# Fp32 opening matmuls, fewer filler matmuls, another order of ko and fo, and shifted batch 1 steps in an attention-and-MoE kernel

## The chip, the cores and the metric

The kernel runs on one core of one Trainium2 chip. The metric is device time in microseconds (us) of that core. Comparisons are of the time of one kernel to that of the kernel before on the same chip in the same rounds. The profiled span (first to last instruction) is some 1.8 us shorter than the device time of the same execution.

## The reference

```python
kv  = einsum('bhsd,bhse->bhde', k, v)          # b 8, h 8, s 576, d 64
out = einsum('bhsd,bhde->bhse', q, kv)
rms = sqrt(mean(out*out, axis=-1, keepdims=True) + 1e-6)
x   = (out / rms * g_norm) -> [4608, 512]
h   = x @ w_in                                 # [512, 2048]
y   = (h * sigmoid(1.702 h)) @ w_out           # [2048, 512]
```

## The kernel before

Tokens go through in nine blocks of 512. Block 0 needs the attention of batch 0 first, and while it runs all weights are still on their way from HBM. The attention of batch b + 1 is spread, as "steps", over the matmuls of block b. GpSimd issues the loads that cast fp32 to fp16, in this order: q, k, v of batch 0 for head pairs 1 to 3 (pair 0 comes through SyncE), `w_in` in five pieces, `w_out` and batch 1's q, k, v interleaved.

Names used below: a pair is two of the eight heads. ko is one of the four blocks of 128 rows of `w_in`, one for each pair; fo is one of the 16 blocks of 128 columns of h. The group is fo 0 to 5 of block 0: 24 matmuls, whose order is part of the change. "The last product" is the scaled attention output of pair 3, which the ko 3 matmuls read. A kv step of batch 1 is k^T v of one pair, for which VectorE first packs k. A gate is the activation on ScalarE. TensorE "stands" by the time that a matmul starts later than 0.216 us after the 512-column matmul before it, which is the spacing in these traces when nothing is waited for (stands at kv steps are counted the same way).

```python
load_w_in(0, 4, 0, 2)      # fo 0-3, ko 0-1
load_w_in(0, 4, 2, KO)     # fo 0-3, ko 2-3   <- "the second w_in half" below
load_w_in(4, GROUP)        # fo 4-5
load_w_in(GROUP, 10)
load_w_in(10, FO)
# ... (cut)
def busy(n):               # filler: zero matmuls into a PSUM tile nobody reads
    for _ in range(n):
        nc.tensor.matmul(idle_ps, kvb[1][:, 0, :],
                         kvb[1].rearrange("p c r -> p (c r)"), start=True, stop=True)

busy(12)                   # the opening
a0.q(0); busy(2); a0.kv(0) # transposes of q, then k^T v, of head pair 0
# ... g_col (cut)
busy(2)
a0.out(0); a0.q(1); a0.kv(1); a0.sums(0)
a0.out(1); a0.q(2); a0.rs(0)
busy(1)
a0.kv(2); a0.sums(1); a0.apply(0)
busy(1)
a0.out(2); a0.rs(1); a0.q(3); a0.kv(3); a0.sums(2); a0.apply(1)
a0.out(3); a0.rs(2); a0.apply(2)
busy(3)
d0 = Hidden(0)             # h = x @ w_in; xT[ko] is what apply(ko) writes
for fo in range(4):        # ko 0; after fo 2: a0.ss(3), a0.apply(3) -> "the last product"
    d0.mm(0, fo, ...)
for ko in (1, 2):
    for fo in range(4): d0.mm(ko, fo)
for ko in range(KO - 1): d0.mm(ko, 4, ps_o, "o")
for fo in range(GROUP - 1): d0.mm(KO - 1, fo)
for ko in range(KO): d0.mm(ko, GROUP - 1, ps_o, "o")
# ... (cut) in block 0's output matmuls, after matmul number n, counted from 0:
at2((25, 27, 42, 43)[c], of(1, "kv", c))
o = (31, 34, 50, 53)[c]
at2(o, of(1, "out", c))
```

## Time and profile before

| | before |
|---|---|
| time, 6 runs beside the changed kernel | 287.00 us median (286.87 to 287.51) |
| profiled span | 284.9 us |
| TensorE busy | 279.1 us |
| v of pair 3, landing | 12.77 us |
| second w_in half, landing | 16.47 us |
| first output matmul of block 0 | 28.73 us |
| first hidden matmul of block 1 | 46.77 us |

From 46.77 us on TensorE waits for no load (one stand of 0.13 us at 47.3). The prediction shows and reads the lines of this profile.

### The profile page before, as it was taken

Reading aid. Unit: us, or ns where it says so; the run is one execution under the profiler, and the core shown is the slowest. Engines: PE = TensorE matmul, PEld = TensorE weight load, DVE = VectorE, ACT = ScalarE, POOL = GpSimd, SP = SyncE. Lnnn points to the kernel's source line nnn. Section 1 sums busy time; section 2 is a strip of 40 time slices with the busy share of each in tenths; the row PEclk is TensorE's granted clock in tenths of the full one; section 3 lists DMA queues with packets and bytes.
Section 4 is the critical chain, followed back from the end, with each engine's and each line's share of the span. In section 5 each row is a group of like instructions: output and inputs, shape, how many; then the busy total and the mean of one; then the engine's idle time right before and its main releaser. Section 6 shows DMA issues by size and latency. Waiting matters only on the chain.

```text
span 284.9 us, 4354 instructions
## 1 busy us (share of the span) xinstructions
PE 279.1 (98%) x1717; PEld 135.1 (47%) x1717; DVE 118.9 (42%) x230; ACT 156.1 (55%) x273; POOL 57.1 (20%) x82
## 2 busy tenths in 40 slices
PE   8899999999999999999999999999999999999995
PEld 2444544455445544554455445544454444444443
DVE  2550666527661657157713852286327400110001
ACT  2697439766575646574458536763666365016400
POOL 8931461111211121112011401130002100000000
PEclk9999999999999999999999999999999999999999
DMA  8999999995589358953797279925401410012022
GB/s 176 200 207 204 205 249 239 242 268 105 122 165 254 60 147 161 242 90 69 224 208 138 38 216 200 184 39 184 83 2 37 120 66 0 0 69 81 0 74 74
DMA packets 54070, 38.76 MB, mean 136 GB/s; under 512 B 31219, under 2 KB 50931, under 8 KB 53923
## 3 DMA queue, kind: packets, MB, share of 16 engines
q0 software_dynamic: 14960, 15.58, 33.5%
q1 hardware_dynamic: 38688, 22.39, 30.2%
q10 hardware_dynamic: 402, 0.52, 0.5%
q8 instruction: 13, 0.21, 0.3%
q14 instruction: 7, 0.05, 0.1%
HBM read 36.73 MB, written 9.44 MB: 162 GB/s over the span
## 4 chain that ended last, share of the span: by engine, by line
PE 93%; POOL 2%; DMA 2%; DVE 1%; issue 0%
PE hT L434 44%; PE o L471 42%; PE kvp L223 3%; DMA vbuf<-in_v_dram 2%; PE outR L287 2%; PE oh L503 1%; POOL kraw L91 1%; PE ss L335 1%; POOL qraw L91 1%; DVE kpad L214 1%; PE outT L255 0%; POOL vbuf L91 0%; PE q L412 0%; PE outT L266 0%; PE idle L558 0%
## 5 line engine op out<-in xcount | busy, mean ns | idle before, releaser
L471 PE MATMUL o<-w_out_sb,gT 128*128 128x512 f16 x560 | 130.7, 379 | 0.0
L443 ACT ACTIVATE gT<-hT 128x512 f16<-128x512 f32 x144 | 84.5, 599 | 76.5 <-PE hT L434 76.4
L434 PE MATMUL hT<-xT,w_in_sb 128*128 128x512 f16 x512 | 116.2, 379 | 0.0
L434 PEld LDWEIGHTS <-w_in_sb 128*128 128x128 f16 x576 | 54.6, 98 | 62.3 <-DMA w_in_sb<-in_moe_w_in_dram 0.5
L471 PEld LDWEIGHTS <-gT 128*128 128x128 f16 x560 | 52.9, 98 | 56.2 <-issue 0.2
L481 DVE COPY osb<-o 128x512 f32<-128x512 f32 x20 | 13.8, 690 | 62.4 <-PE o L471 62.4
L319 POOL TENSOR_TENSOR x<-xr,g_all 128x512 f16<-128x512 f32 x12 | 15.2, 1270 | 71.2 <-DVE xr L312 47.2
L214 DVE COPY kpad<-kraw 64x576 f16<-64x576 f16 x56 | 25.0, 446 | 2.0 <-DMA kraw<-in_k_dram 0.7
L298 DVE TENSOR_REDUCE sum<-sq 128x8 f32<-128x512 f16 x24 | 15.8, 679 | 19.9 <-ACT sq L295 19.9
L236 DVE CAST kvb<-kvp 64x128 f16<-64x128 f32 x28 | 8.1, 288 | 36.5 <-PE kvp L223 36.4
L312 DVE TENSOR_TENSOR xr<-outR,sum 128x512 f32<-128x512 f32 x24 | 15.5, 686 | 11.1 <-ACT sum L309 11.1
L112 POOL DMA_DIRECT2D kraw<-in_k_dram x16 | 9.9, 624 | 48.8 <-DVE kpad L214 42.8
L112 POOL DMA_DIRECT2D vbuf<-in_v_dram x16 | 9.7, 608 | 33.9 <-PE kvp L223 29.3
L319 DVE TENSOR_TENSOR x<-xr,g_all 128x512 f16<-128x512 f32 x12 | 15.2, 1267 | 0.7
L295 ACT ACTIVATE sq<-outR 128x512 f16<-128x512 f32 x24 | 13.6, 591 | 2.0 <-PE outR L287 1.6
L223 PEld LDWEIGHTS <-kpad 128*128 128x128 f16 x252 | 11.0, 98 | 7.0 <-DVE kpad L214 0.9
L434 PE MATMUL hT<-x_rem,w_in_sb 128*128 128x512 f16 x64 | 14.0, 379 | 0.0
L275 ACT ACTIVATE sq<-outT 128x512 f16<-128x512 f32 (+1 forms) x16 | 7.7, 481 | 10.4 <-PE outT L255 9.0
L481 ACT COPY osb<-o 128x512 f32<-128x512 f32 x15 | 8.7, 581 | 6.3 <-DMA out_dram<-osb 6.3
L223 PE MATMUL kvp<-vbuf,kpad 128*128 128x64 f16 x252 | 11.9, 193 | 0.1
L308 ACT ACTIVATE sum<-sum,eps_t 128x16 f32<-128x16 f32 x12 | 3.7, 308 | 15.0 <-DVE sum L298 14.9
L337 ACT ACTIVATE ln<-ss,eps_t 128x512 f32<-128x512 f32 (+1 forms) x16 | 9.4, 586 | 4.3 <-PE ss L335 4.1
(62 smaller groups left out, 141.5 us busy)
## 6 DMA issues: line engine op xcount, KB each, us to landing
qf<-in_q_dram SPq DMA_DIRECT2D x5, 1024.0 KB, 9.0
out_dram<-osb SPq DMA_DIRECT2D x10, 512.0 KB, 2.9
kraw<-in_k_dram POOLq DMA_DIRECT2D x12, 288.0 KB, 6.9
vbuf<-in_v_dram POOLq DMA_DIRECT2D x12, 288.0 KB, 5.5
w_out_sb<-in_moe_w_out_dram POOLq DMA_DIRECT2D x3, 512.0 KB, 14.4
out_dram<-osb SPq DMA_DIRECT2D x6, 192.0 KB, 5.5
qf<-in_q_dram POOLq DMA_DIRECT2D x1, 1024.0 KB, 11.1
out_dram<-osb SPq DMA_DIRECT2D x1, 1024.0 KB, 3.8
```

Source lines behind the costliest of these rows:

```text
L112: nc.gpsimd.dma_start(out=raw[n][l * PH : (l + 1) * PH, c0:c1, 0 : NH * D], in_=srcs[n][b].rearrange("(c l) (p j) d -> l p c (j d)", l=2, ...
L214: nc.vector.tensor_copy(out=kpad[r, c, :, l * D : (l + 1) * D], in_=kraw[r, c, 0 : NH * D].rearrange("p (j d) -> p j d", j=NH),)
L223: nc.tensor.matmul(self.kvp[:, c, :], kpad[:, c, j, :], vbuf[:, c, j * D : (j + 1) * D], start=(j == 0), stop=(j == NH - 1),)
L295: nc.scalar.activation(sq, t, AFT.Square)
L298: nc.vector.tensor_reduce(out=self.sum2[:, j % 2, :], in_=sq.rearrange("p (h d) -> p h d", h=H), op=ALU.add, axis=mybir.AxisListType.X,)
L312: nc.vector.tensor_mul(xr[:, i], self.o[j + i].rearrange("p (h d) -> p h d", h=H), s2[:, i, :].unsqueeze(2).to_broadcast([P, H, D]),)
L319: (nc.vector if i else nc.gpsimd).tensor_mul(self.x16[:, j + i, :].rearrange("p (h d) -> p h d", h=H), xr[:, i], g_all.unsqueeze(1).to_bro ...
L337: nc.scalar.activation(ln[:, 0:n], t[:, 0:n], AFT.Ln, bias=eps_t, scale=1.0 / D)
L434: nc.tensor.matmul(self.h[fo], w_in_sb[:, ko, fo * P : (fo + 1) * P], self.x[:, ko], start=(ko == 0), stop=(ko == KO - 1),)
L443: nc.scalar.activation(self.gT[:, fo, :], self.h[fo], AFT.Gelu_apprx_sigmoid)
L471: nc.tensor.matmul(os[mo], gT[:, fo, mo * P : (mo + 1) * P], w_out_sb[:, fo, :], start=(fo == 0), stop=(fo == FO - 1),)
L481: copy(osb[:, mo, :], os[mo])
```

## The change

Its intent, as far as the code tells: to release TensorE's clock with fewer instructions, to take out filler, to run each fo of the first group in a simpler order, and to give batch 1's kv matmuls more time to be fed.

```diff
+    zeros = const.tile([P, SM], F32)
+    nc.vector.memset(zeros, 0.0)
...
-    busy(12)
+    for _ in range(3):
+        nc.tensor.matmul(idle_ps, zeros[:, 0:P], zeros, start=True, stop=True)
...
     a0.rs(0)
-    busy(1)
     a0.kv(2)
     a0.sums(1)
     a0.apply(0)
-    busy(1)
     a0.out(2)
...
-    busy(3)
+    busy(1)
...
-    for ko in (1, 2):
+    for ko in range(1, KO):
         for fo in range(4):
             d0.mm(ko, fo)
-    for ko in range(KO - 1):
-        d0.mm(ko, 4, ps_o, "o")
-    for fo in range(GROUP - 1):
-        d0.mm(KO - 1, fo)
-    for ko in range(KO):
-        d0.mm(ko, GROUP - 1, ps_o, "o")
+    for fo in range(4, GROUP):
+        for ko in range(KO):
+            d0.mm(ko, fo, ps_o, "o")
...
-                at2((25, 27, 42, 43)[c], of(1, "kv", c))
-                o = (31, 34, 50, 53)[c]
+                at2((27, 28, 42, 43)[c], of(1, "kv", c))
+                o = (32, 35, 50, 53)[c]
```

## The prediction

> **What bounds the kernel now.** I read the page first (busy shares, clock, chain), then the chain in order of time, then the waits, and last the timeline of the first 48 us, where the change lies.
>
> ```profile
> span 284.9 us, 4354 instructions
> PE 279.1 (98%) x1717; PEld 135.1 (47%) x1717; DVE 118.9 (42%) x230; ACT 156.1 (55%) x273; POOL 57.1 (20%) x82
> ...
> PE 93%; POOL 2%; DMA 2%; DVE 1%; issue 0%
> ```
>
> TensorE is busy 98% of the span and is 93% of the chain that ended last. Of the 576 hidden and 560 output matmuls nothing changes, so the change can only win or lose idle or filler time of TensorE, and only where that time is on the chain. The chain in order of time says where that is not so:
>
> ```profile
> 7.23 5.54 DMA vbuf<-in_v_dram
> 12.90 0.40 PE kv L372 x12
> 13.68 0.39 PE outT L255
> 14.07 0.65 PE idle L558 x3
> 14.71 0.65 PE hT L434 x3
> ```
>
> Up to 12.9 us the chain is not TensorE but GpSimd issuing loads and the landing of the last v block of batch 0 (issued 7.23, landed 12.77). The twelve opening zero matmuls are not in it. After 12.9 us the three zero matmuls are in it, but see what follows them:
>
> ```profile
> 1.27 4.92 PE L558 MATMUL idle<-kvb 128*128 128x512 f16 x12 [1.27 <-DVE one_t L185]
> 6.16 0.31 PEld L389 LDWEIGHTS <-qraw 96*64 96x64 f16 x12 [0.49 <-ACT qraw L549]
> 12.90 0.38 PE L372 MATMUL kv<-vbuf,kraw 96*64 96x64 f16 x12 [0.70 <-DMA vbuf<-in_v_dram]
> 16.51 0.76 PEld L434 LDWEIGHTS <-w_in_sb 128*128 128x128 f16 x5 [0.35 <-DMA w_in_sb<-in_moe_w_in_dram]
> 17.00 0.75 DVE L349 SCALAR_TENSOR_TENSOR xT<-outT,g_col,rs 128x512 f16<-128x512 f32 x1 [0.88 <-ACT rs L343]
> 35.52 0.32 PEld L223 LDWEIGHTS <-kpad 128*128 128x128 f16 x9 [0.36 <-DVE kpad L214]
> 36.47 0.32 PEld L223 LDWEIGHTS <-kpad 128*128 128x128 f16 x9 [0.58 <-DVE kpad L214]
> ```
>
> At 6.16 the first transposes wait for ScalarE's cast of q; at 12.90 TensorE has stood 0.70 us for a load; at 16.51 a weight load waits for the second half (ko 2 and 3) of the first w_in load. The trace has that load landing at 16.469, issued at 8.615 from GpSimd, with nothing before it that waits on TensorE. At 36.47 the second kv step of batch 1 waits for VectorE's packing of k. No later stretch shows TensorE waiting, so a shift there reaches the end one for one.
>
> **What the Trainium skill says.** (1) TensorE: Matmul & The Clock Gate, Part 1, "What's actually happening": the array runs at 1.2 GHz after idleness and 2.4 GHz after about one busy window of 3.4 us. This case agrees: the opening matmuls start 0.426 us apart up to 5.09, the one at 5.514 takes 0.300, and later 512-column matmuls start 0.216 apart. (2) FP8 and Floating Point Precision, "TensorE Precision Notes": true fp32 takes four passes. The trace of before has fp32 matmuls only for g_ps: two instructions recorded as four load and four matmul records, one column wide, so it shows the split into two records but not the time. (3) VectorE: DVE Perf Modes, "Zero memsets can be issued as uint32 (trn2)": one cycle per element. Here 256 words took 0.27 us and 1152 words 1.02, so about 0.84 ns a word more: it agrees. (4) DMA: Bandwidth & Descriptors, "Queues, rings and completion order": descriptors are consumed in ring order. The landings of GpSimd's loads do come in order of issue here (14.07, 16.47, 17.11, 19.64, 23.37 for the five w_in loads), so moving TensorE's work should not move them.
>
> **Part 1, the opening.** Twelve fp16 matmuls of 512 columns go; three fp32 ones of four passes come: 12 x 512 column steps either way, so the same array time. The new memset of 512 words (estimate from the two measured ones: 0.27 + 256 x 0.84 ns = 0.48 us) stands where the 0.27 us memset stood, so TensorE starts near 1.50 instead of 1.27. If the clock still doubles near 5.69 (0.173 us into the matmul at 5.514, from its 0.300), 4.19 us cold cover 5028 of 6144 steps and the other 1116 take 0.47 us warm: end 6.16, just where the q transposes start today on ScalarE's cast. Cost on the chain: nothing, and even 0.5 us late would fit in the 0.70 us stand at 12.90 plus the fillers taken out below.
>
> **Part 2, single fillers before kv 2 and out 2.** 0.43 us of TensorE goes, ahead of the 12.77 landing: nothing on the chain.
>
> **Part 3, three fillers to one after out 3.** out 3 starts at 13.68 as before (DMA-led). The hidden matmuls start at 14.12 instead of 14.55, just after the landing at 14.07. Three of them end at 14.77; the sum matmul for pair 3 then waits for ScalarE's square (14.23 + 0.60 = 14.83, about 0.05 to start) and goes at 14.88, not 15.20: 0.32 us earlier. Log, exp and the last product follow: log 15.62 to 15.30, exp 16.34 to 16.02, product 17.00 to 16.68, ending near 17.43. TensorE does fo 3 and ko 1 (five matmuls) from 15.10 to 16.17 and then stands until the landing: ko 2 starts at 16.515 **as before**. The 0.43 us taken out turns into a wait for w_in.
>
> **Part 4, the order of ko and fo.** From 16.515 on both orders have 16 matmuls of the group left. Before, ko 3 came after seven of them, at 18.04, and the last product, done at 17.75, was hidden. Now ko 3 comes after four, which would be at 17.39; the last product is there at 17.43 + 0.05 = 17.48. So a stand of 0.09 us: the group ends 0.09 us later (its last matmul at 19.86 instead of 19.76). fo 4 needs the load of 17.11, in time. The gates start earlier (about 17.95 instead of 18.45, behind the 1.28 us table load) but ScalarE is not what ends last here. The later loads for fo 6 and 10 (19.64, 23.37) are in before 20.07 and 23.64. Sum of the front: **+0.09 us**.
>
> **Part 5, batch 1 steps.** Before: the kv step of pair 0 after step 25 loses 35.521 - 35.486 = 0.035 us; pair 1 after step 27 could go at 36.226 and goes at 36.478 when its packing is done: 0.252 us lost. Now two more output matmuls (2 x 0.216) come ahead of pair 0, which then starts at 35.92 without a wait; after one more, pair 1 could go at 36.39 and still waits to 36.478, 0.084 us. Everything from there has one more output matmul behind it at the same moment. The out step moves from 31 to 32, so four matmuls still cover the two copies of kv (36.95 to 37.54), and it still goes at 37.615. kv of pairs 2 and 3 would go near 40.42 with their v landed at 40.09 and their packing done at 40.09: still fed. Gain: **-0.216 us**.
>
> **Sum.** +0.09 - 0.216 = -0.13 us of 287.01: **286.9 us**.
>
> **Rivals.** (a) The fp32 opening is slower than four passes, or doesn't release the clock: the start would slip. For: no duration of an fp32 512-column matmul is in this trace. Against: the replacement of 12 by 3 is just the skill's factor of four. Absorbed up to about 0.7 us; if each took twice as long, some 4 us would go, of which over 3 us reach the end: 290. (b) The taken-out 0.86 us of fillers (four at 0.216) come back in full, with part 5: 287.01 - 0.86 - 0.22 = 285.9. For: three of the five fillers concerned are in the chain at 14.07. Against: the wait at 16.51 for a load that TensorE doesn't lead. (c) ko 3 waits longer, because the sum of pair 3 isn't earlier than today (15.20): the product would end at 17.75, ko 3 at 17.80, 0.41 us lost in the front and 287.2 in all. (d) The later kv steps meet another wait (v for pairs 2 and 3 lands 0.3 us ahead of need): the gain of part 5 goes, 287.1.
>
> **Range and chances.** All but (a) lie between 285.9 and 287.2, with the three timed runs of before 0.25 us apart. I weigh (b) little. Range 286.4 to 287.4. Two per cent is 5.7 us: only a gross form of (a) reaches it. Faster by over 2%: 0.003; within 2%: 0.987; slower by over 2%: 0.01.
>
> **What would show it.** In the changed trace: six fp32 matmul records in the opening, each near 0.85 us apart while cold, ending about 6.2; the kv matmuls of pair 3 still at 12.90 behind v; a weight load at 16.5 behind w_in with a longer idle than 0.35; the last product near 16.7; a short gap of TensorE before ko 3; then the kv step of pair 1 with under 0.1 us of stand. Wrong if the opening ends after 7 us, if ko 2 starts well before 16.5, or if the first output matmul comes earlier than in before (28.73).

## The result, and the profile after

The changed kernel took 286.89 us (median of 6, 286.75 to 287.15), the one before 287.00 us in the same rounds. The ratio is 0.9994, 95% interval 0.9981 to 1.0007: the same. (A ratio is the mean time of one kernel's fast runs over that of the other's of the same rounds, so not quite the ratio of the medians quoted.) A difference of 0.11 us lies far inside that interval, so the sum can't be checked by time; its terms can be checked in the traces, where each is a shift between two events of one execution.

The page of the changed kernel, span, TensorE row and chain by engine:

```profile
span 285.0 us, 4335 instructions
PE 278.8 (98%) x1707; PEld 134.9 (47%) x1707; DVE 119.2 (42%) x231; ACT 156.2 (55%) x273; POOL 57.2 (20%) x82
...
PE 93%; DMA 3%; POOL 3%; issue 0%; DVE 0%
```

TensorE has 0.3 us less to do, and the span is no shorter. The chain that ended last, in order of time, says why (changed kernel; start, duration, what):

```profile
8.01 0.72 POOL w_in_sb L168
8.73 7.80 DMA w_in_sb<-in_moe_w_in_dram
16.53 0.05 issue
16.58 5.48 PE hT L436 x24
```

Before, the chain ran through the landing of v at 12.77 and then through TensorE. Now the landing of the second w_in half at 16.53 is in it, and all TensorE work before 16.58 has dropped out of the chain. Of the 0.43 us of fillers taken out after out 3, 0.09 became a stand at the sum of pair 3 and 0.28 a longer stand ahead of ko 2 (0.304 us, before 0.020).

The lines of the timeline that answer to those shown of before (start, duration, engine, line, operation; in brackets the engine's idle time before it and what ended it):

```profile
1.54 5.06 PE L570 MATMUL idle<-zeros 128*128 128x512 f32 x6 [1.54 <-DVE zeros L152]
6.54 0.45 PE L391 MATMUL q<-ident,qraw 96*64 96x96 f16 x12
13.02 0.38 PE L374 MATMUL kv<-vbuf,kraw 96*64 96x64 f16 x12 [0.62 <-DMA vbuf<-in_v_dram]
16.57 0.76 PEld L436 LDWEIGHTS <-w_in_sb 128*128 128x128 f16 x5 [0.63 <-DMA w_in_sb<-in_moe_w_in_dram]
16.78 0.75 DVE L351 SCALAR_TENSOR_TENSOR xT<-outT,g_col,rs 128x512 f16<-128x512 f32 x1 [0.54 <-ACT rs L345]
23.80 0.33 PEld L436 LDWEIGHTS <-w_in_sb 128*128 128x128 f16 x3 [0.40 <-DMA w_in_sb<-in_moe_w_in_dram]
36.74 0.32 PEld L225 LDWEIGHTS <-kpad 128*128 128x128 f16 x9 [0.23 <-DVE kpad L216]
```

The weight load at 16.57 waits 0.63 us where it waited 0.35. The last product starts at 16.78 instead of 17.00. At 23.80 a matmul now stands for its load: the last w_in load (fo 10 to 15) landed at 23.76, not at 23.37, when only the weight load had waited (0.20 us at 23.41). Only one kv wait is left, at 36.74, of 0.23 us for the weight loads, where there were two of 0.36 and 0.58.

TensorE's shift at the first hidden matmul of block 1, in parts, each from starts of single instructions:

| part | before | after | difference |
|---|---|---|---|
| second w_in half lands | 16.469 | 16.532 | +0.063 |
| from there to the group's last matmul | 3.294 | 3.420 | +0.126 (stand at ko 3 of 0.129) |
| from there to the first output matmul | 8.966 | 9.044 | +0.078 (stand at fo 10 of 0.068) |
| from there to block 1 | 18.044 | 17.830 | -0.214 |
| first hidden matmul of block 1 | 46.773 | 46.826 | +0.053 |

Rest of the kernel: 234.496 us before to the last matmul's start, 234.498 after. So this execution lost 0.053 us; of that, 0.063 and most of 0.078 are landings that fell later in it.

### The profile page after: what moved, and what is told of

The parts are those of the page before. It is cut to its first block, busy times and chain, and to the rows that moved or that the text cites. A ratio compares the mean times of both kernels' runs of the same rounds, so it can differ in the third digit from the quotient of the medians.

```text
span 285.0 us, 4335 instructions
## 1 busy us (share of the span) xinstructions
PE 278.8 (98%) x1707; PEld 134.9 (47%) x1707; DVE 119.2 (42%) x231; ACT 156.2 (55%) x273; POOL 57.2 (20%) x82
## 4 chain that ended last, share of the span: by engine, by line
PE 93%; DMA 3%; POOL 3%; issue 0%; DVE 0%
PE hT L436 43%; PE o L473 42%; DMA w_in_sb<-in_moe_w_in_dram 3%; PE kvp L225 3%; PE outR L289 2%; PE oh L505 1%; POOL qraw L91 1%; POOL kraw L91 1%; POOL vbuf L91 1%; PE ss L337 1%; PE q L414 0%; PE outT L268 0%; PE outT L257 0%; POOL w_in_sb L168 0%; POOL ident L154 0%
```

## The experiments

Each kernel was built and timed beside the kernel before in five rounds; all gave correct results. "Low clock" counts the executions whose mean granted TensorE clock was 0.996 or less.

| run | median us (range) | before, same rounds | ratio, 95% interval | low clock |
|---|---|---|---|---|
| changed, first rounds | 286.89 (286.75 to 287.15) | 287.00 | 0.9994, 0.9981 to 1.0007 | 0 of 6 |
| e1_opening | 287.21 (286.68 to 289.87) | 287.38 | 1.0009, 0.9978 to 1.0039 | 0 of 6 |
| e2_front | 287.33 (287.06 to 288.84) | 287.38 | 1.0010, 0.9988 to 1.0032 | 2 of 6 |
| e3_steps | 286.84 (286.54 to 287.07) | 287.38 | 0.9985, 0.9970 to 1.0000 | 0 of 5 |
| e4_old_order | 286.87 (286.54 to 288.49) | 287.38 | 0.9995, 0.9974 to 1.0016 | 1 of 6 |
| e5_changed_again | 286.84 (286.61 to 288.69) | 287.03 | 1.0004, 0.9984 to 1.0024 | 1 of 6 |
| e6_singles_back | 286.91 (286.54 to 287.27) | 287.03 | 0.9996, 0.9983 to 1.0009 | 0 of 5 |
| e7_no_fillers | 286.99 (286.37 to 287.53) | 287.03 | 0.9998, 0.9986 to 1.0010 | 1 of 6 |
| e8_combined | 287.10 (286.80 to 287.54) | 287.03 | 1.0005, 0.9993 to 1.0017 | 0 of 5 |
| e9_cut_loads | 286.65 (286.47 to 287.32) | 286.93 | 0.9991, 0.9979 to 1.0004 | 0 of 5 |
| e10_no_opening | 288.40 (287.32 to 289.36) | 286.93 | 1.0042, 1.0021 to 1.0063 | 0 of 6 |
| e11_six | 288.76 (288.09 to 289.21) | 286.93 | 1.0056, 1.0042 to 1.0070 | 0 of 5 |
| e12_fillers_only | 286.88 (286.80 to 288.16) | 286.93 | 1.0002, 0.9987 to 1.0017 | 1 of 6 |

Only e10 and e11 differ from before beyond their interval. The rest is read from traces. What makes single traces hard to compare is the landings: the gap between the landings of the first and second w_in half was 2.2 to 2.8 us in five traces (before, changed, e5, e6, e12) and 1.2 to 1.3 us in the other seven in which that load was whole (e1 to e4, e7, e10, e11), with no pattern by kernel that I could find: the changed kernel had the late landing both times. So I measure stands and stretches inside one trace.

### e1: the opening alone

```diff
-    busy(12)
+    for _ in range(3):
+        nc.tensor.matmul(idle_ps, zeros[:, 0:P], zeros, start=True, stop=True)
     # and the memset of zeros
```

> The kernel before with the fp32 opening alone. Theory (the opening lies in the slack before the landing of v): six records about 0.85 us apart, the first q transposes 0.0 to 0.5 us later than the 6.16 us of before, but the kv matmuls of pair 3 still within 0.1 us of the landing of their v, and from there nothing moved other than by landings; time ratio to before 1.000 within 0.001. Rival (the start is on the path): the shift of the transposes is still there at the kv matmuls of pair 3, after their v has landed, and the time goes up by the same 0.3 to 0.5 us.

Six records, the cold ones 0.853 us apart. q started at 5.92, earlier than before and not later as expected, because this time the clock was released at 4.81 us and not at 6.05 as in the changed kernel. kv of pair 3 started 0.136 us after its v landed, over the 0.1 expected, but as before (0.135). The form of the opening doesn't reach the end: theory held in what matters. One execution of 289.87 us with its clock at 0.999 has no explanation here; its trace was not taken.

### e2: fillers and order alone

```diff
-    busy(1)        # ahead of kv 2
-    busy(1)        # ahead of out 2
-    busy(3)
+    busy(1)
     # and the new order of ko and fo
```

> The kernel before with the five fillers cut to one and the new order of ko and fo alone; the opening and the batch 1 steps are those of before. Theory (the landing of the second w_in half leads ko 2): the filler time turns into a stand of TensorE in front of ko 2, the first ko 2 weights load within 0.06 us of that landing, ko 3 stands 0.08 to 0.15 us for the last product; from landing to the end of the group 3.55 to 3.65 us against 3.51 in before; time 0.0 to 0.2 us above before. Rival (fillers come back): ko 2 starts 0.3 us or more before 16.5 and the time falls by 0.4 us or more.

Neither theory nor rival described this trace. Stretches of it: length, TensorE busy (instructions), granted clock, DMA share, GB/s.

```profile
10.00:12.00 2.00, 1.49 (x27) 1.00 1.31 199
12.00:13.60 1.60, 0.90 (x14) 0.99 1.21 185
13.60:17.00 3.40, 3.33 (x19) 0.50 1.32 202
17.00:19.00 2.00, 2.00 (x10) 1.00 1.24 208
```

From 13.58 to 16.99 us the clock stood at half. The kernel before has 2.00 us busy in the stretch from 10 to 12 and a clock of 1.00 in all of these. So the fillers may have a use that I had not seen: in this execution the clock fell just after the stretch in which they were gone, and the span was 287.0 us. That they would have kept the clock, this trace alone doesn't show. The second w_in half landed early here (16.09), and TensorE didn't wait for it; ko 3 stood 0.446 us for the last product.

### e3: the batch 1 steps alone

```diff
-    at2((25, 27, 42, 43)[c], of(1, "kv", c));  o = (31, 34, 50, 53)[c]
+    at2((27, 28, 42, 43)[c], of(1, "kv", c));  o = (32, 35, 50, 53)[c]
```

> The kernel before with the two kv and two out steps of batch 1 shifted, nothing else. Theory: the stand ahead of the kv matmuls of pair 1 falls from 0.25 to about 0.08 us and that of pair 0 from 0.035 to 0, so the stretch from the first output matmul to the first hidden matmul of token block 1 is 0.216 us shorter than the 18.04 us of before; time 0.1 to 0.3 us less. Rival (the gain is lost at a later step, such as kv of pair 2 waiting for its v): that stretch stays at 18.04 us within 0.05.

The waits of the weight loads for VectorE's packing (total us, times, longest), in the kernel before:

```profile
PEld L223 <- DVE kpad L214: 0.9, 2, 0.6
```

and in e3:

```profile
PEld L223 <- DVE kpad L214: 0.2, 1, 0.2
```

Stands of the matmuls: 0.083 us at pair 1 and none at pair 0. The stretch from first output matmul to block 1 was 17.828 us: 0.216 us less than 18.044, as computed. The theory held to the hundredth of a microsecond in the trace. The medians differ by 0.54 us, more than the steps can give; that is within the noise of these rounds.

### e4: the changed kernel with the old order

```diff
-    for ko in range(1, KO):                      # all of fo 0-3, then fo 4 and 5
+    for ko in (1, 2): ...                        # ko 3 of fo 0-3 after ko 0-2 of fo 4
```

> The changed kernel with the old order of ko and fo put back: everything else as changed. Theory (the new order exposes the last product): the stand ahead of ko 3 of 0.13 us in the changed kernel goes to 0, the group ends 3.5 us after the landing of the second w_in half instead of 3.6, unless the load for fo 4 lands too late for its new place 4 matmuls after ko 2 starts (it landed 0.64 us after the ko 2 load in before and 0.96 in the changed kernel; fo 4 comes 0.87 us after ko 2 starts). Time 0.0 to 0.2 us less than the changed kernel. Rival: the order was changed because the fo 4 load is late: then TensorE stands there instead and nothing is won, or up to 0.1 us lost.

ko 3 no longer stood. But fo 4 stood 0.068 us for its load (landed 17.15), fo 10 stood 0.075 us for its load (23.39), and an output matmul stood 0.123 us at 37.42 for the piece of w_out with fo 8 to 11 (37.38). The group ended 6.72 us after the landing of v (before 6.99, changed 7.07), yet the stretch from output matmul to block 1 grew to 17.951. Part of the gain was given back at the next landing. e3 is the closer comparison: it has the same order and the same steps, all five fillers, and an early second half too. From the landing of v to the group's end e4 is 0.25 us shorter (6.718 against 6.964), and to the first hidden matmul of block 1 only 0.04 (33.720 against 33.758). So with an early half, 0.25 of the 0.43 us of fillers after out 3 did come back, and was then lost at the next landings. Theory held on ko 3, and the rival's wait came too, smaller.

### e5: the changed kernel again

> The changed kernel once more, untouched, to have it beside the others on one chip. In the front-only run the clock fell to half for one 3.4 us window near 13 to 17 us in the profiled execution (mean clock 0.993), and 1 of 6 runs of the old-order one had 0.994. Theory (the removed fillers also kept the array busy enough): the changed kernel shows it too, 0 to 3 of 6 runs at a mean clock of 0.996 or less and 1 to 2 us longer, the rest at 286.7 to 287.2. Where the second w_in half lands early (1.3 us after the first, as in the last four runs), theory for the front: ko 3 still starts 0.05 us after the last product, so the group ends 7.0 to 7.1 us after the landing of v for pair 3, as in before (6.99). Rival (only the landing held it): the group ends 6.75 us or less after it.

One of six executions had a clock of 0.994 and took 288.69 us; the other five lay at 286.61 to 287.08. So the changed kernel has the loss of clock too. In the profiled execution the second w_in half landed late, at 16.63, 4.06 us after v, and TensorE stood 0.717 us for it:

```profile
16.68 1.69 PE L436 MATMUL hT<-xT,w_in_sb 128*128 128x512 f16 x7 [0.55 <-DMA w_in_sb<-in_moe_w_in_dram]
```

(The bracket counts from the modelled end of the matmul before.) ko 3 did not stand at all, since the last product was done before ko 2 was through. The early-landing case that the expectation speaks of didn't come up here. It came in e7.

### e6: the two single fillers put back

```diff
     a0.rs(0)
+    busy(1)
     a0.kv(2)
     ...
+    busy(1)
     a0.out(2)
```

> The changed kernel with the two single fillers ahead of kv 2 and out 2 put back. Theory (those two hold the clock through the stretch of 10 to 13 us): no run at a mean clock of 0.996 or less, and in the trace nothing from the landing of v for pair 3 on moved by more than 0.05 us against the changed kernel. Rival (the loss of clock comes from the two fillers taken out after out 3, or from chance): the low-clock runs are as frequent as in the changed kernel.

No low clock in five. From the landing of v to the end of the last product 4.646 us, in the changed kernel 4.646: the two fillers cost nothing, as the landing of v comes after them. Later landings did move things by more than the 0.05 us expected: an output matmul stood 0.146 us at 37.59 for w_out, and the stretch to block 1 was 17.973 us (17.830). Five executions don't prove that the clock is safe: at one in six, none of five would come up by chance two times in five.

### e7: no filler after the opening

```diff
     a0.q(0)
-    busy(2)
     a0.kv(0)
     ...
-    busy(2)
     a0.out(0)
     ...
-    busy(1)
     d0 = Hidden(0)
```

> The changed kernel with every filler after the opening taken out (two pairs and the last one), so that the suspected loss of clock is exaggerated; the opening of three fp32 stays. Theory: at least 2 of 6 runs at a mean clock of 0.996 or less and 1 us or more longer than the others; median 287 to 289. Rival (fillers don't matter for the clock once it is released): no such run, and the time within 0.2 us of the changed kernel.

One low clock of six, not two or more, and that execution took 287.53 us, not 1 us more: my expectation missed. More filler taken out didn't make the loss more frequent. The trace showed the front with an early second w_in half (15.68), in a line of the timeline:

```profile
17.84 1.46 PE L436 MATMUL hT<-xT,w_in_sb 128*128 128x512 f16 x6 [0.27 <-DVE xT L351]
```

ko 3 waits for the last product, 0.434 us by matmul starts, and the group ends 7.075 us after v landed. So with the new order the front has two ceilings: the landing, and, when that is early, the last product. The freed time is gone either way.

### e8: a version from the findings so far

```diff
     # changed kernel, single fillers back, old order of ko and fo, and
-    load_w_in(0, 4, 2, KO)
+    load_w_in(0, 4, 2, 3)
+    load_w_in(0, 4, 3, KO)
-    load_w_in(10, FO)
+    load_w_in(10, 12)
+    load_w_in(12, FO)
-    at2((27, 28, 42, 43)[c], of(1, "kv", c));  o = (32, 35, 50, 53)[c]
+    at2((27, 29, 42, 43)[c], of(1, "kv", c));  o = (33, 36, 50, 53)[c]
```

> A version made from the findings: the changed kernel with the single fillers back, the old order of ko and fo, the second w_in half cut in two loads and the last w_in load cut in two (fo 10-11, fo 12-15), and kv of pair 1 one step later (outs too). Theory: the stand ahead of the kv matmuls of pair 1 is under 0.02 us (0.085 in the changed kernel), no stand at fo 10, the group ends 0.2 to 0.3 us sooner after v of pair 3 landed than in before (6.99), so 0.4 to 0.6 us under before in all and no run at a low clock: 286.3 to 286.7. Rival: the load for fo 4 (17.1 to 17.5) takes the place of ko 3 as the stand and the front gains 0.1 or less.

The kv stand of pair 1 went to 0.000 and fo 10 didn't wait. But fo 4 stood 0.292 us for its load, and this line came up:

```profile
37.73 0.59 PE L475 MATMUL o<-w_out_sb,gT 128*128 128x512 f16 x2 [0.31 <-DMA w_out_sb<-in_moe_w_out_dram]
```

An output matmul stands 0.469 us by matmul starts for fo 8 of w_out, landed at 37.69. The group ended 6.945 us after v: the rival was right, and 0.3 us of gain in the steps ran into the next load. No faster than before.

### e9: two more loads cut

```diff
-    load_w_in(4, GROUP)
+    load_w_in(4, 5)
+    load_w_in(5, GROUP)
-            load_w_out(8, 12)
+            load_w_out(8, 10)
+            load_w_out(10, 12)
```

> The combined version with two more loads cut in two: w_in for fo 4-5 and w_out for fo 8-11. In the combined run the TensorE gains ran into the landing of w_out fo 8-11 (stand of 0.469 us at 37.73) and of w_in fo 4-5 (0.292 at 17.33). Theory (one landing after another paces the first 48 us, and the first half of a cut load lands earlier by about half of the time that load takes): both stands fall below 0.1 us, the group ends 0.2 us or more sooner after v of pair 3 than the 6.99 us of before, and the stretch from first output matmul to token block 1 is 17.72 to 17.80 us (17.83 in the changed kernel): 286.3 to 286.7, 0.3 to 0.6 us under before. Rival (cutting only moves the wait to the next landing, or costs on the queue): one of the stands is still 0.2 us or more, or another of that size appears, and the time stays within 0.2 us of before.

The trace is that of the slowest of the five executions (287.32 us). The two stands fell to under 0.02 us (fo 4) and 0.129 us (at 38.34, for the second half of the cut w_out load). The group ended 6.64 us after v. But the kv matmuls of pair 2 now stood 0.214 us, and the waits of TensorE name it:

```profile
PE kvp L228 <- DMA vbuf<-in_v_dram: 0.2, 1, 0.2
```

v of batch 1's second half landed at 40.79, 0.13 us before that step; later, in block 1, another kv step stood 0.318 us at 57.0. The median, 286.65, is the lowest and 0.28 us under before; its interval includes 1. The stretch to block 1 was 18.073 us, not 17.72 to 17.80. So the rival was right about the wait that moves on, and the theory about the group's end and, nearly, the two stands (0.129 is over its 0.1).

### e10: no opening at all

```diff
-    for _ in range(3):
-        nc.tensor.matmul(idle_ps, zeros[:, 0:P], zeros, start=True, stop=True)
```

> The changed kernel without its three opening matmuls. Theory (the opening only releases the clock, its form doesn't matter): the matmuls of batch 0's attention run at half clock (two zero matmuls 0.427 us apart), the clock is released late, between 9 and 18 us, kv of pair 3 starts 0.2 us or more after its v landed, and the time is 1 to 3 us above the changed kernel. Rival (the opening isn't needed): kv of pair 3 starts within 0.15 us of the landing and the time is within 0.3 us of the changed kernel.

The timeline of TensorE:

```profile
7.07 1.03 PE L560 MATMUL idle<-kvb 128*128 128x512 f16 x2
14.65 0.52 PE L374 MATMUL kv<-vbuf,kraw 96*64 96x64 f16 x12
16.44 1.26 PE L436 MATMUL hT<-xT,w_in_sb 128*128 128x512 f16 x3
```

The trace is of a slow execution of the six (289.22 us). Zero matmuls are 0.40 to 0.43 us apart, kv of pair 3 starts 1.83 us after its v (landed 12.82), and the clock is released at 17.34. Time 288.40, ratio 1.0042: the opening is worth 1.5 us. With e1, which changed the form alone, it is the release, and not the form, that counts.

### e11: six fp32 matmuls

```diff
-    for _ in range(3):
+    for _ in range(6):
```

> The changed kernel with six opening fp32 matmuls in place of three, to find the slack of the opening. Theory (array time of four passes at the released clock, 0.43 us a record, and a slack of about 0.7 us before v of pair 3): the twelve records end near 8.8 us, the q transposes start 2.2 to 2.6 us later than the 6.2 to 6.6 of the changed kernel, kv of pair 3 starts 1.2 to 2.0 us after the landing of its v instead of 0.13, and 0.9 to 1.8 us of that reach the end. Rival (the front has far more slack): less than 0.4 us reaches the end.

```profile
1.54 7.82 PE L570 MATMUL idle<-zeros 128*128 128x512 f32 x12 [1.54 <-DVE zeros L152]
9.29 0.45 PE L391 MATMUL q<-ident,qraw 96*64 96x96 f16 x12
14.79 0.35 PE L374 MATMUL kv<-vbuf,kraw 96*64 96x64 f16 x12
```

Records are 0.853 us apart cold and 0.430 after the release at 6.41. q starts 2.75 us later than in the changed kernel, a little more than expected because the release came later than assumed. kv of pair 3 starts 2.03 us after its v instead of 0.135. On the clock of the trace it starts at 14.793 instead of 13.018, 1.775 us later (its v landed 0.12 us sooner): the slack of the opening is 2.753 - 1.775 = 0.98 us. The time grew by 1.83 us over before (medians), a hair over the upper end expected. What goes beyond the slack reaches the end.

### e12: the fillers alone

```diff
-    busy(1)        # ahead of kv 2
-    busy(1)        # ahead of out 2
-    busy(3)
+    busy(1)
```

> The kernel before with the five fillers cut to one, its order, opening and steps kept: the fillers by themselves. So far a mean clock of 0.994 or less came in 5 of 30 executions of kernels without the two single fillers and in none of 43 with them whose clock is on record. Theory (those fillers guard the clock, and the freed time is taken by landings): 0 to 3 of 6 runs at 0.996 or less, 1 to 2 us longer; the others within 0.3 us of before; in the trace the kv and fo 4 or fo 10 stands show where the freed 0.43 us went. Rival (the freed time is kept): the runs at full clock 0.3 us or more under before.

Here the second w_in half landed late, at 16.68. Weight loads:

```profile
16.72 0.78 PEld L434 LDWEIGHTS <-w_in_sb 128*128 128x128 f16 x5 [0.86 <-DMA w_in_sb<-in_moe_w_in_dram]
```

TensorE stood 0.527 us at ko 2 (before 0.020), and that is where the freed time went, not to the later stands that I expected. The group ended 3.295 us after the landing, before 3.294. That isolates Part 3 of the prediction for a late second half: fillers taken out with nothing else change nothing from the landing on. One of six executions had a clock of 0.994 and 288.16 us; the other five took 286.80 to 286.92.

### What the clock counts say

The kernels that lack the two single fillers and keep an opening of ordinary length (changed twice, e2, e4, e7, e12) had 6 low-clock executions of 36. Those that have them (before, e1, e3, e6, e8, e9) had none of 59. I formed the idea on e2 and e4, so the fair count starts after them: 3 of 18 (e5, e7, e12) against 0 of 37 (before in two calls, e6, e8, e9). If both kinds were alike, all three would fall in the first kind with a chance of (18 x 17 x 16) / (55 x 54 x 53) = 3%. That fillers guard the clock is therefore likely and not proved. It is at odds that e7 had no more of it than e5, and that e10 and e11, which also lack the singles, had none of 11; I left them out for their opening, and with them the 3% becomes 8%. Nor do the counts separate the two singles from the two fillers taken out after out 3: the kernels with the singles and without those two (e6, e8, e9) have only 15 executions.

The half-clock window was seen in one trace only, and this trace holds a hint. In e2's clock records the first stretch at full clock lasts 6.827 us and the one at half clock 3.413, half of it. Cut every trace from its release on in steps of that length, up to 24 us: the step just ahead of the fall is the emptiest of all, with 2.23 us of TensorE busy; the next emptiest is in e3, which kept its clock (2.36). In e2 and then e3:

```profile
10.17:13.58 3.41, 2.23 (x39) 1.00 1.26 192
4.86:8.27 3.41, 2.36 (x35) 1.00 1.24 186
```

The two singles would have added some 0.43 us to e2's step (an estimate, two at 0.216). Where a step falls depends on when the clock was released, so this would fit a loss in some executions only; with one fall traced it is not shown.

## Why the prediction was right

- **Part 1, the opening.** Right in effect. The memset took 0.485 us (0.48 worked out; 64, 256, 512 and 1152 words took 0.112, 0.272, 0.485 and 1.018, so 0.83 ns a word, and whether that is one cycle, as the page that the prediction cites has it, no run here shows) and TensorE started at 1.54 (1.50). Records came 0.853 us apart. The end near 6.16 didn't come true: q started at 6.54, since the clock was released at 6.05 and not at 5.69. No run here controls the release time: it fell between 4.5 and 7.2 us in the thirteen traces that have an opening. The slack absorbed it, as argued; e11 put it at 0.98 us (0.70 plus part of the fillers was the estimate), and e10 showed that the release is what the opening is for.
- **Part 2, the single fillers.** Right on the median time (e6, 4.646 us with and without them), blind to the clock. In one of the twelve executions of the changed kernel the loss came: 288.69 us against a median of 286.82 us of the other five of those rounds.
- **Part 3, three fillers to one.** Right, and isolated by e12: ko 2 starts with the landing, and the freed time is a wait. That needs a late second half, which the prediction took from one trace; only five of twelve traces had it, so that the changed kernel's did is luck. In e4 and e7 ko 2 started 0.84 and 0.86 us after an early landing, and waited for nothing. The start of the last product, 16.68 predicted, was 16.78 with v 0.11 us later.
- **Part 4, the order.** Right kind, small by 0.04: 0.129 us of stand at ko 3 against 0.09 predicted; e4 took it away. But the stand is the gap between two things that move apart: the landing and the last product. With the new order it was 0 in e5, 0.129 in the changed kernel's trace, 0.241 in e6, and 0.43 to 0.45 in e7 and e2, as the second half landed earlier after v. So the closeness to 0.09 is luck in part. When the half is early the last product holds the front, which the prediction named only as rival (c), and for another reason.
- **The assumption in Part 4 that failed** is that the later loads "are in before 20.07 and 23.64": the landing for fo 10 came at 23.76 in the changed trace, and TensorE stood 0.068 us. GpSimd's loads landed in order of issue in every trace; their times did not hold.
- **Part 5, the steps.** Right to 0.002 us in two traces (17.830 and 17.828 against 17.828 worked out), and to 0.005 in four more with these steps (e5, e7, e10, e11). In e4 and e6 a wait for w_out at 37.4 to 37.6 made it 17.951 and 17.973.
- **The sum**, -0.13 us, agrees with the -0.11 us of medians, but no timing here resolves it (e5 gave -0.19 by medians, and a ratio of 1.0004), so that they agree is chance. The profiled pair gave +0.053, all of the difference to the prediction being landings and the 0.04 of Part 4.
- **Rivals.** (a) is refuted by 0.853 us a record, and its size was too large: e11 has an opening of twice the work, and q came 2.75 us later, not 4, and the end 1.83 us, not over 3. (b) is refuted by e12 for a late second half, and by e4 against e3 for an early one; (c) came in a form with another cause; (d) didn't come in the changed kernel, and came in e9, once the front was 0.35 us faster (group end 6.64 us after v against 6.99).

So the change moved little because the first 41 us are, to within some tenths of a microsecond, paced by a queue of loads. In the kernel before, seven of them are used 0.05 to 0.7 us after they land: the w_in pieces after 0.48, 0.05, 0.28, 0.34 and 0.18 us, w_out for fo 8 after 0.66, v of batch 1's second half after 0.55. A saving of TensorE is kept only as far as the next landing leaves room: the 0.21 us of Part 5 fitted into the 0.55 us ahead of v's use and stayed, the others did not.

## What to carry to other kernels

Before taking out filler on a chain, look for the next landing behind it: when a load that TensorE doesn't lead lands less than the saving later, the saving turns into a wait, and cutting one load only shows the next. Filler may also hold the clock; the loss showed here in about a sixth of the executions without the fillers, and not in a median: list the clock of every execution. Where a change is worth less than the spread of the timing, compare stretches between two events inside the traces; 0.216 us could be read there to the hundredth.

## What the Trainium skill lacked or had wrong

- FP8 and Floating Point Precision, "TensorE Precision Notes", gives four passes for fp32 and no time. Here a 128x512 fp32 matmul is recorded as two weight loads and two matmuls, each record 0.853 us cold and 0.430 us warm, so 1.71 and 0.86 us an instruction: four times the 0.427 and the 0.216 us of an fp16 one. The statement holds.
- TensorE: Matmul & The Clock Gate, Part 1, ties the fall to half clock to an idle window of about 3.4 us, and its closing table asks for "No PE-idle gaps >~3µs between matmul bursts". In e2 the clock fell at 13.58 us although no two matmul starts between 10.2 and 13.7 us were more than 0.91 us apart. So the absence of long gaps is not enough. The same page does tell, further down, of a kernel that lost the clock through frequent short idle times, with no figure for how much idle time it takes; nor does any run here settle that.
- The same page: "The warm-up budget is ~3.4 µs of time, not a number of matmuls." Here the release came 3.0 to 5.8 us after the first opening matmul (thirteen traces), so a budget of 3.4 us is too small for most; its remark that the window is free-running fits the spread.
- Reading a trace (no page read here has it): the mean granted clock is counted from the first release on. e10 shows 0.999, though its array ran cold until 17.34 us.
- DMA: Bandwidth & Descriptors, "Queues, rings and completion order", says in which order one DMA engine consumes descriptors, and that completion need not follow the order of issue. Here GpSimd's loads landed in order of issue in all fourteen traces. It has nothing on the spread: the same two w_in halves landed 1.2 to 2.8 us apart.
